# Batch 0's attention ahead of the first gate, value means on TensorE, weight subtraction on VectorE, and due times set from behind, in an attention and gated-expert kernel on one core

## The chip, the core and the metric

The kernel runs on one core of a Trainium2 chip. A core has five engines, each with its own queue of instructions that it runs in order: TensorE (PE, matmuls, with its weight loads shown as PEld), VectorE (DVE), ScalarE (ACT), GpSimd (POOL) and SyncE (SP, which here issues all DMAs). They share the on-chip memory SBUF; matmul results land in PSUM. Engines wait for each other by semaphores. The metric is the device time of one execution in microseconds; the number before is the median of three runs.

## The reference

Four batches of 768 tokens, 8 heads of 64. Each query attends to the keys within 16 positions of it and to 24 block summaries (maximum of 32 keys, mean of 32 values). The attention output, 512 features a token, then goes through a token mix, a squared-ReLU expert and a sigmoid gate.

```python
k_sum = k.reshape(B, H, nb, block, D).max(axis=3)
v_sum = v.reshape(B, H, nb, block, D).mean(axis=3)
mask_l = np.abs(pos[:, None] - pos[None, :]) < window
scores_s = scale * np.einsum('bhsd,bhnd->bhsn', q, k_sum) + np.log(block)
scores_all = np.concatenate([np.where(mask_l, scale * q @ kT, -1e9), scores_s], axis=-1)
a = softmax(scores_all)
x = a @ np.concatenate([v, v_sum], axis=2)
...
xk = mu_k * x + (1.0 - mu_k) * x_prev
xr = mu_r * x + (1.0 - mu_r) * x_prev
k = np.maximum(xk @ w_k, 0.0)
v = k * k @ w_v
r = 1.0 / (1.0 + np.exp(-(xr @ w_r)))
return r * v
```

## The kernel before

Work is cut into half batches of 384 tokens, written (b, hf), and four pairs of heads, p.

**Attention.** `load_set` issues the loads of a pair: keys `kt`, queries `qt`, value windows `vw`, and values with features on partitions, `vt`. `summaries` makes the block maxima of the keys on DVE (`kg`, `ks`, copied into `kt`), and the value means: a sum over `vt` on DVE (L327), a transpose on PE (L330), a scaled copy on ACT (`vm`, L332), and a DMA that spreads `vm` over the windows (L339). For batch 0 the loads and copies are made for each half separately, for the other batches once for both. `unit` is one pair and one half: 24 small score matmuls (L361), six times mask with row minimum on DVE (L372) and exponential with row sum on ACT (L376), the reciprocal of the sums on DVE (L382, L383), six scalings on POOL (L388), two groups of three transposes on PE (L395), each copied by ACT into `pts` (L399), 24 small value matmuls (L408), and a copy into `xt` on DVE (L419). There are 32 units, eight a batch.

**Weights.** They arrive as 64-bit words. For each of 20 blocks (4 of `w_r`, 8 each of `w_k` and `w_v`), `weight` loads `st` (L235), scales one word on ACT or POOL (L243, L246), takes bits from the other in two steps on DVE (L252, L255), joins them on DVE into `wc` (L260), casts that on ACT to the high part (L272), and subtracts on POOL to get the low part (L274). Products of a high and low operand are three matmuls: high-high, high-low, low-high.

**Tokens.** For each half, `mixes` makes high and low parts `xs` for the gate and then for the expert, four pairs each: ACT multiplies (L431), DVE adds (L434), ACT casts (L437), DVE subtracts (L439). `gate` is three tiles of 12 matmuls (L452 to L454) with a sigmoid on ACT each (L459). `experts` does eight steps j: `first` (`e1`, 12 matmuls at L472, which need weight block `wk` j; ReLU, square and a cast, then `kl` by subtraction on DVE, L487) and `second` (`e2`, 9 matmuls at L498, which need `wv` j, `kh` and `kl`). The last `e2` is followed by the product with the gate (L520) and the stores (L524).

**What sets the order.** Everything is first noted as an operation with an engine, a length from the table `LENGTH`, a due time and the buffers that it uses. `Plan.schedule` then plays the program forward: on each engine it takes, of the operations that can start, the one with the earliest due time, and so fixes the order of every engine's queue and which buffer of a pool each one gets. Nothing is reordered on the chip. Due times are written at each operation as offsets from the times of the half: the first gate is due at `T0`, each half `PERIOD` later, `e1` steps `STEP` apart. The four units of half (0,0) are due before the first gate, those of half (0,1) after it, and the eight units of the next batch during the two halves of this one.

```python
    for hf in range(2):
        for p in range(NPAIR):
            due = (16000 + 6000 * p) if hf == 0 else T0 + 4000 + 6000 * p
            e = load_set(0, p, hf * HW, HW, due)
            summaries(0, p, e, due)
            unit(0, p, hf, e, due)
```

## Time and profile before

| | |
|---|---|
| median of three runs | 493.21 us (491.12 to 852.7) |
| the profiled execution | 493.59 us, span 491.8 us |
| PE busy | 444.9 us, 90% of the span, 3376 matmuls |
| DVE busy | 295.0 us, 60% |
| ACT busy | 293.6 us, 60% |
| POOL busy | 119.8 us, 24% |
| chain that ended last | PE 70%, POOL 8%, ACT 7%, DVE 6%, DMA 5%, issue 3% |
| DMA | 42.82 MB read, 6.29 MB written, mean 106 GB/s |

The span is the time between the first and the last instruction in the trace. Busy times are averages over stages that have different limits, so the stages are read apart. The page cuts the span into 40 slices of 12.3 us; the digits are tenths of busy time. The lines for PE, DVE and POOL are these:

```profile
PE   1476988669889999999999999999999999999996
...
DVE  3879789999847676424677565526764654323223
...
POOL 0655346684512410001324120002343100000000
```

PE has its low slices at the left; DVE is at its fullest there, from the sixth slice to the tenth, and POOL too.

### The profile page before, as it was taken

How to read it: one execution, taken by the hardware profiler on the slowest of the kernel's cores; microseconds unless marked ns; L12 is line 12 of the kernel's file. 1: busy time of each engine (PE TensorE's matmuls, PEld its weight loads, DVE VectorE, ACT ScalarE, POOL GpSimd, SP SyncE). 2: the span in 40 equal slices, each digit the busy share in tenths (PEclk: the TensorE clock that was granted, in tenths of full speed). 3: DMA queues.
4: the chain of work that ended last, by engine and by line, in shares of the span. 5: the costliest groups of instructions: out<-in, count | busy, mean ns of one | idle time of the engine just before them, and what ended most of it. 6: DMA issues, size and time to landing. Idle time of an engine off the chain costs nothing.

```text
span 491.8 us, 9346 instructions
## 1 busy us (share of the span) xinstructions
PE 444.9 (90%) x3376; PEld 372.1 (76%) x3376; DVE 295.0 (60%) x914; ACT 293.6 (60%) x804; POOL 119.8 (24%) x228
## 2 busy tenths in 40 slices
PE   1476988669889999999999999999999999999996
...
DVE  3879789999847676424677565526764654323223
...
POOL 0655346684512410001324120002343100000000
...
GB/s 248 343 237 201 189 192 221 200 260 2 135 100 113 129 134 73 40 0 24 165 171 171 171 50 65 1 0 149 116 63 64 11 0 65 0 2 64 1 0 64
DMA packets 25501, 52.06 MB, mean 106 GB/s; under 512 B 2672, under 2 KB 12656, under 8 KB 25456
## 3 DMA queue, kind: packets, MB, share of 16 engines
...
HBM read 42.82 MB, written 6.29 MB: 100 GB/s over the span
## 4 chain that ended last, share of the span: by engine, by line
PE 70%; POOL 8%; ACT 7%; DVE 6%; DMA 5%; issue 3%; SPq 1%; DVEq 0%; POOLq 0%; ACTq 0%
PE mm L498 24%; PE mm L472 22%; POOL y L388 4%; PE mm L452 4%; PE mm L454 4%; PE mm L453 4%; PE av L408 4%; PE sc L361 4%; PE pt L395 4%; DMA kt<-in_k 3%; ACT y L376 2%; DVE we L255 1%; DMA vw<-vm 1%; POOL wv_l L274 1%; ACT L376 1%
## 5 line engine op out<-in xcount | busy, mean ns | idle before, releaser
L388 POOL TENSOR_SCALAR y<-y,rc 128x120 f32<-128x120 f32 x192 | 82.6, 449 | 249.0 <-DVE rc L383 197.1
L472 PE MATMUL mm<-xs,wk_h 128*128 128x384 f32 x512 | 102.3, 342 | 5.6 <-ACT r L478 4.3
L472 PEld LDWEIGHTS mm<-xs,wk_h 128*128 128x128 f32 x512 | 90.3, 189 | 10.7 <-ACT r L478 5.0
L376 ACT ACTIVATE y<-y,mn 128x120 f32<-128x120 f32 x192 | 73.8, 386 | 22.9 <-DVE mn L372 22.7
L478 ACT ACTIVATE r<-mm 128x384 f32<-128x384 f32 x64 | 31.3, 489 | 88.0 <-PE mm L472 87.6
L498 PE MATMUL mm<-wv_l,kh 128*128 128x512 f32 x192 | 76.9, 401 | 4.1 <-POOL wv_l L274 4.1
L498 PE MATMUL mm<-wv_h,kh 128*128 128x512 f32 x192 | 79.3, 413 | 0.0
L485 DVE CAST kh<-r 128x384 fp32r<-128x384 f32 x56 | 20.9, 374 | 88.7 <-ACT r L480 88.1
L498 PE MATMUL mm<-wv_h,kl 128*128 128x512 f32 x192 | 61.0, 413 | 0.3 <-DVE kl L487 0.3
L472 PE MATMUL mm<-xs,wk_l 128*128 128x384 f32 x256 | 55.3, 338 | 0.0
L439 DVE TENSOR_TENSOR xs<-xa,xs 128x384 fp32r<-128x384 f32 x64 | 36.2, 587 | 27.3 <-ACT xs L437 27.2
L372 DVE CUSTOM_DVE_ANT_0 y<-sc,mask_sb 128x120 f32<-128x120 f32 x192 | 44.1, 275 | 12.5 <-PE sc L361 11.9
L361 PE MATMUL sc<-kt,qt 64*64 64x120 f32 x768 | 33.1, 307 | 17.6 <-DVE kt L336 15.2
L472 PEld LDWEIGHTS mm<-xs,wk_l 128*128 128x128 f32 x256 | 45.5, 188 | 0.2
L395 PE MATMUL pt<-ident_sb,y 128*120 128x128 f32 x192 | 38.2, 308 | 8.0 <-POOL y L388 2.9
L498 PEld LDWEIGHTS mm<-wv_l,kh 128*128 128x128 f32 x192 | 36.6, 191 | 11.0 <-POOL wv_l L274 5.1
L361 PEld LDWEIGHTS sc<-kt,qt 64*64 64x64 f32 x768 | 24.1, 154 | 26.4 <-DVE kt L336 16.7
L498 PEld LDWEIGHTS mm<-wv_h,kh 128*128 128x128 f32 x192 | 36.8, 192 | 7.0 <-issue 0.6
L498 PEld LDWEIGHTS mm<-wv_h,kl 128*128 128x128 f32 x192 | 34.9, 192 | 8.6 <-DVE kl L487 0.8
L431 ACT ACTIVATE xa<-xt,om_sb 128x384 f32<-128x384 f32 x64 | 36.7, 608 | 7.6 <-DVE xt L419 6.6
L487 DVE TENSOR_TENSOR kl<-r,kh 128x384 fp32r<-128x384 f32 x64 | 37.1, 579 | 5.5 <-ACT kh L483 1.9
L434 DVE SCALAR_TENSOR_TENSOR xa<-xt,mu_sb,xa 128x384 f32<-128x384 f32 x64 | 38.1, 622 | 3.3 <-ACT xa L431 3.3
...
## 6 DMA issues: line engine op xcount, KB each, us to landing
...
```

The lines of the kernel that those rows point to most:

```text
L361: nc.tensor.matmul(sc[h].t[cs, i, 0:NK], qt.t[hs, w * QW:(w + 1) * QW], kt.t[hs, w * KB:w * KB + NK], start=True, stop=True,)
L372: op("DVE", "mask", due - 9000 + 300 * (NSL * h + i), lambda h=h, i=i, var=var: nc.vector.tensor_tensor_reduce(out=y[h].t[:, i, :], in0=sc ...
L376: op("ACT", "exp", due - 8500 + 300 * (NSL * h + i), lambda h=h, i=i: nc.scalar.activation(y[h].t[:, i, :], y[h].t[:, i, :], AF.Exp, bias= ...
L388: op("POOL", "norm", due - 5500 + 300 * (NSL * h + i), lambda h=h, i=i: nc.gpsimd.tensor_scalar(out=y[h].t[:, i, :], in0=y[h].t[:, i, :], ...
L395: nc.tensor.transpose(out=pt[h].t[0:NK, i * P:(i + 1) * P], in_=y[h].t[:, i, :], identity=ident_sb)
L431: op("ACT", "mixa", t - 4000, lambda xt=xt, xa=xa, p=p: nc.scalar.activation(xa.t, xt.t[:, lo:lo + HT], AF.Copy, scale=om_sb[:, which, p:p ...
L434: op("DVE", "mixd", t - 3300, lambda xt=xt, xa=xa, p=p: nc.vector.scalar_tensor_tensor(out=xa.t, in0=xt.t[:, 1 + lo:1 + lo + HT], scalar=m ...
L439: op("DVE", "sub", t - 1800, lambda xa=xa, xh=xh, xl=xl: nc.vector.tensor_tensor(out=xl.t, in0=xa.t, in1=xh.t.bitcast(F32), op=ALU.subtrac ...
L472: nc.tensor.matmul(ps.t[:, 0:HT], w[:, j, p, :], x[p][s].t, start=(n == 0), stop=(n == 11))
L478: op("ACT", "relu", due + 2200, lambda: nc.scalar.activation(r.t, ps.t[:, 0:HT], AF.Relu), reads=[(ps, 0)], writes=[(r, 0)])
L487: op("DVE", "sub", due + 3700, lambda: nc.vector.tensor_tensor(out=kl.t, in0=r.t, in1=kh.t.bitcast(F32), op=ALU.subtract), reads=[(r, 0), ...
L498: nc.tensor.matmul(acc[t].t, a.t[:, t * P:(t + 1) * P], w[:, j, :], start=start, stop=stop)
```

## The change

It has six parts.

1. **Batch 0 as a whole ahead of the first gate.** Each pair of batch 0 is loaded once for both halves, as in the other batches, and all eight units are due before the first gate (`GATES[0] - 2000`, 4000 ns apart). Queries come in a DMA of their own for each unit. In SP's list value windows go ahead of the mask.
2. **Value means of batch 0 by PE.** Twelve matmuls with a small constant matrix `pool_sb` (one more load) accumulate the 24 block means straight from the value windows, into a `mm` buffer. POOL first fills the rows of the windows that hold the means with zeros, since the matmuls read them. The load `vt`, the sum on DVE and the transpose are gone for batch 0; in the other batches they stay, with a `st` buffer for `vt`.
3. **The low part of a weight on DVE** in place of POOL, 20 subtractions of 128x512.
4. **Either of two engines.** An operation may name a second engine; the planner gives it to the one that ends it first. So the first step of a mix may go to POOL, the copy of the block maxima to POOL, the copy out of `av` to ACT, the cast of `kh` to ACT, the scaling of a weight to ACT or POOL.
5. **The gate of half (0,1) between steps of half (0,0).** Its `xs` are made early, and its three tiles stand in the program ahead of `e1` steps 1, 2 and 3.
6. **Dues from behind, and new numbers.** Only the operations of PE, the copies out of `av`, the last products and the stores keep a due time of their own; every other takes the earliest due time of what needs it, less its length and a slack. Loads aren't issued earlier than 15000 ns ahead of their due. The table of lengths is new, and the pools are cut differently (three `kt` in place of two, four `y` in place of six, three `pts` in place of four; windows and `xt` share twelve `vx`).

PE's matmuls are otherwise the same ones, in another order, and the number of activation table loads on ACT is the same, 24.

```diff
-LATENCY = dict(PE=260, DVE=130, ACT=150, POOL=150, SP=0)
-DMA_NS_PER_BYTE = 1 / 300.0
+TAIL = dict(PE=0, DVE=85, ACT=95, POOL=0, SP=0)
+LATENCY = dict(PE=260, DVE=110, ACT=110, POOL=150, SP=0)
+DMA_NS_PER_BYTE = 1 / 290.0
 DMA_FIXED = 2000
-T0 = 40000
+GATES = (36000, 46000)
 PERIOD = 52000
 STEP = 4800
+SLACK = 300
+EARLY = 15000
+FIRST = 4000
+UNITS = 6000
+BETWEEN = 1, 2, 3
...
+        ways = {eng: (LENGTH.get(cost, 0), emit)}
+        if other:
+            ways[other[0]] = (LENGTH[other[1]], other[2])
+        o = Op(len(self.ops), ways, due, bufs, size)
...
+        for o in reversed(self.ops):
+            own = 1.0e9 if o.due is None else o.due
+            wait = DMA_FIXED + o.size * DMA_NS_PER_BYTE if "SP" in o.ways else min(c for c, _ in o.ways.values()) + SLACK
+            o.due = min([own] + [s.due - wait for s in o.succ])
...
-                    start, need, ok = max(at, now), {}, True
+                    start, need, ok = max(at, now, o.due - EARLY if e == "SP" else 0), {}, True
...
+                    if any(max(start, engines[f]) + c < start + o.ways[e][0] for f, (c, _) in o.ways.items() if f != e):
+                        continue
...
-        kt=tiles("kt", 2, [P, KL]), qt=tiles("qt", 2, [P, S]), vw=tiles("vw", 2, [NK, NW, P]),
-        vt=tiles("vt", 1, [P, S]), kg=tiles("kg", 2, [P, 49]), ks=tiles("ks", NPAIR + 1, [P, NS]),
-        vs=tiles("vs", 2, [P, NS]), vm=tiles("vm", NPAIR + 1, [NS, P]),
-        y=tiles("y", 6, [P, NSL, NK]), mn=tiles("mn", 6, [P, NSL]), sm=tiles("sm", 4, [P, 2 * NSL]),
-        rc=tiles("rc", 4, [P, 2 * NSL]), pts=tiles("pts", 4, [NK, NSL, P]),
-        xt=tiles("xt", 7, [P, S + 1]), z=tiles("z", 2, [P, NTT, DM]),
-        xs=tiles("xs", 16, [P, HT], F32R), xa=tiles("xa", 4, [P, HT]),
-        r=tiles("r", 2, [P, HT]), kh=tiles("kh", 2, [P, HT], F32R), kl=tiles("kl", 2, [P, HT], F32R),
-        st=tiles("st", 3, [P, 1024], U32), wc=tiles("wc", 2, [P, 512], U32), we=tiles("we", 1, [P, 512], U32),
+        kt=tiles("kt", 3, [P, KL]), qt=tiles("qt", 4, [P, HT]), vx=tiles("vx", 12, [P, S + 1]),
+        kg=tiles("kg", 2, [P, 49]), ks=tiles("ks", 2, [P, NS]),
+        vs=tiles("vs", 1, [P, NS]), vm=tiles("vm", 4, [NS, P]),
+        y=tiles("y", 4, [P, NSL, NK]), mn=tiles("mn", 4, [P, NSL]), sm=tiles("sm", 3, [P, 2 * NSL]),
+        rc=tiles("rc", 3, [P, 2 * NSL]), pts=tiles("pts", 3, [NK, NSL, P]),
+        z=tiles("z", 6, [P, DM]), xa=tiles("xa", 4, [P, HT]),
+        xs=tiles("xs", 16, [P, HT], F32R), r=tiles("r", 2, [P, HT]),
+        kh=tiles("kh", 2, [P, HT], F32R), kl=tiles("kl", 2, [P, HT], F32R),
+        st=tiles("st", 3, [P, 1024], U32), we=tiles("we", 1, [P, 512], U32), wc=tiles("wc", 2, [P, 512], U32),
...
+        op("ACT", "wscale", None, scale_act, reads=[(st, 0)], writes=whole, other=("POOL", "wscale_p", scale_pool))
...
-        op("POOL", "sub_p", due - 1500, lambda: nc.gpsimd.tensor_tensor(
...
+        op("DVE", "wsub", None, lambda: nc.vector.tensor_tensor(
             out=dst_l, in0=wc.t.bitcast(F32), in1=dst_h.bitcast(F32), op=ALU.subtract),
-           reads=[(wc, 0), ((name, i), "h")], writes=[((name, i), "l")])
-
-
-    xts, key_sums, value_sums = {}, {}, {}
-
-    def load_set(b, p, w0, nw, due):
-
-        half = 1 if w0 else 0
-        e = dict(kt=buf("kt"), qt=buf("qt"), vw=buf("vw"), vt=None if half else buf("vt"), w0=w0, nw=nw)
-        first = w0 * KB
-        end = KL if half or nw == NW or b == 0 else first + nw * KB + 2 * WINDOW
-        kt, qt, vw = e["kt"], e["qt"], e["vw"]
-        cuts = [first, HW * KB, KL] if (b, p, w0) == (0, 0, 0) else [first, end]
+           reads=[*whole, ((name, i), "h")], writes=[((name, i), "l")])
...
+        op("DVE", "kcopy", None, copies(nc.vector), reads=[(ks, 0)], writes=[(kt, "s")],
+           other=("POOL", "kcopy_p", copies(nc.gpsimd)))
+        if b == 0:
+            tp = buf("mm")
+
+            for x in vw:
+                op("POOL", "fill", None, lambda x=x: nc.gpsimd.memset(x.t[QW:KB, 0:S], 0.0), writes=[(x, "b")])
+
+            def means():
+                for w in range(NW):
+                    nc.tensor.matmul(
+                        tp.t[0:NS, 0:P], pool_sb[:, NS - 2 - 2 * w:2 * NS - 2 - 2 * w], windows(vw[w // HW])[:, w % HW, :],
+                        start=(w == 0), stop=(w == NW - 1))
+
+            op("PE", "vpool", None, means, reads=[(x, y) for x in vw for y in "abc"] + [*POOLM], writes=[(tp, 0)])
...
+        for x in vw:
+            op("SP", "load", None, lambda x=x: nc.sync.dma_start(
+                out=windows(x)[QW:KB], in_=vm.t.unsqueeze(1).broadcast_to([NS, HW, P])),
+               reads=[(vm, 0)], writes=[(x, "b")], size=NS * HW * 512)
...
+        op("SP", "load", None, lambda: nc.sync.dma_start(out=qt.t, in_=q[b, p, :, hf * HT:(hf + 1) * HT]),
+           writes=[(qt, 0)], size=P * HT * 4)
...
+            op("POOL", "tiny", None, lambda: nc.gpsimd.memset(xt.t[:, 0:1], 0.0), writes=[(xt, "z")])
...
+           other=("ACT", "evac_a", lambda: nc.scalar.copy(out=xt.t[:, 1 + hf * HT:1 + (hf + 1) * HT], in_=av.t)))
...
+               other=("POOL", "mixa_p", lambda xt=xt, xa=xa, p=p: nc.gpsimd.tensor_scalar(
+                   out=xa.t, in0=xt.t[:, lo:lo + HT], scalar1=om_sb[:, which, p:p + 1], scalar2=1.0,
+                   op0=ALU.mult, op1=ALU.mult)))
...
+    def gate_tile(b, hf, x, z, t):
+        ps = buf("mm")
+        ts = slice(t * P, (t + 1) * P)
+
+        def products():
+            for p, (xh, xl) in enumerate(x):
+                nc.tensor.matmul(ps.t, xh.t[:, ts], wr_h[:, p, :], start=(p == 0), stop=False)
+                nc.tensor.matmul(ps.t, xh.t[:, ts], wr_l[:, p, :], start=False, stop=False)
+                nc.tensor.matmul(ps.t, xl.t[:, ts], wr_h[:, p, :], start=False, stop=(p == NPAIR - 1))
+
+        op("PE", "gate", gate_due(b, hf) + 2800 * t, products, reads=[(a, 0) for pair in x for a in pair]
+           + [(("wr", i), s) for i in range(NCK) for s in "hl"], writes=[(ps, 0)])
+        op("ACT", "sigmoid", None, lambda: nc.scalar.activation(z[t].t, ps.t, AF.Sigmoid),
+           reads=[(ps, 0)], writes=[(z[t], 0)])
...
-            if b == 0 and hf == 0:
-                op("ACT", "cast", due + 3200, lambda: nc.scalar.copy(out=kh.t, in_=r.t), reads=[(r, 0)], writes=[(kh, 0)])
-            else:
-                op("DVE", "khv", due + 3200, lambda: nc.vector.tensor_copy(out=kh.t, in_=r.t),
-                   reads=[(r, 0)], writes=[(kh, 0)])
-            op("DVE", "sub", due + 3700, lambda: nc.vector.tensor_tensor(
+            op("DVE", "khv", None, lambda: nc.vector.tensor_copy(out=kh.t, in_=r.t),
+               reads=[(r, 0)], writes=[(kh, 0)], other=("ACT", "cast", lambda: nc.scalar.copy(out=kh.t, in_=r.t)))
...
+            for work in between.get(j, ()):
+                work()
...
-    for hf in range(2):
-        for p in range(NPAIR):
-            due = (16000 + 6000 * p) if hf == 0 else T0 + 4000 + 6000 * p
-            e = load_set(0, p, hf * HW, HW, due)
-            summaries(0, p, e, due)
-            unit(0, p, hf, e, due)
...
+    for p in range(NPAIR):
+        e = load_set(0, p)
+        for h in range(2):
+            unit(0, p, h, e, GATES[0] - 2000 - (7 - 2 * p - h) * FIRST)
+    tokens = {}
+    for n in range(2 * B):
+        b, hf = divmod(n, 2)
+        if n not in tokens:
+            tokens[n] = mixes(b, hf, 1), [buf("z") for _ in range(NTT)]
+            for t in range(NTT):
+                gate_tile(b, hf, *tokens[n], t)
+        between = {}
+        x = mixes(b, hf, 0)
+        if n == 0:
+
+            tokens[1] = mixes(0, 1, 1), [buf("z") for _ in range(NTT)]
+            between = {j: [lambda t=t: gate_tile(0, 1, *tokens[1], t)] for t, j in enumerate(BETWEEN)}
+        experts(b, hf, x, tokens[n][1], between)
...
+    means = np.zeros((NK, 2 * NS - 2), np.float32)
+    means[WINDOW:WINDOW + BLOCK, NS - 2] = 1.0 / BLOCK
+    means[WINDOW + BLOCK:QW, NS - 1] = 1.0 / BLOCK
+    means[KB:KB + WINDOW, NS - 1] = 1.0 / BLOCK
```

What this does to the order of the queues, at three places. First PE around the first gate (`sc` scores, `pts` and `av` values, `y` and `pt` transposes, `mm` with `wr` the gate, with `wk` the first `e1`). Before, where the last work ahead of the gate, the end of the gate and the first `e1` stand:

```order
L408 MATMUL av0_150<-pts0_102,vw0_65 64x64
...
L361 MATMUL sc1_148<-kt0_61,qt0_63 64x120 x2
L452 MATMUL mm0_151<-wr_h_163,xs0_115 128x512
L453 MATMUL mm0_151<-wr_l_164,xs0_115 128x512
...
L454 MATMUL mm2_153<-wr_h_163,xs7_122 128x512
L395 MATMUL pt0_149<-ident_sb_156,y4_86 120x128 x3
L472 MATMUL mm3_154<-xs8_123,wk_h_159 128x384
...
L395 MATMUL pt0_149<-ident_sb_156,y5_87 120x128 x3
```

and now, with the second gate's first tile that follows the first `e1`:

```order
L430 MATMUL pt0_146<-ident_sb_153,y2_91 120x128 x3
L430 MATMUL pt0_146<-ident_sb_153,y3_92 120x128 x3
...
L443 MATMUL av0_147<-pts0_103,vx10_78 64x64
L489 MATMUL mm0_148<-wr_h_160,xs0_116 128x512
L490 MATMUL mm0_148<-wr_l_161,xs0_116 128x512
...
L510 MATMUL mm3_151<-xs14_130,wk_l_157 128x384
L396 MATMUL sc0_144<-kt1_62,qt0_64 64x120 x2
...
L489 MATMUL mm0_148<-wr_h_160,xs0_116 128x512
...
L510 MATMUL mm1_149<-xs8_124,wk_h_156 128x384
```

Ahead of the gate stood seven scores, ten groups of transposes and five values; now eight scores, sixteen groups, eight values and the four mean products stand there, and the transposes of batch 0 that stood among the first `e1` are gone from there.

Second DVE in the middle of the weights (`we` and `wc` the steps of a block, `y` a mask). Before:

```order
L252 TENSOR_SCALAR we_146<-st_141 128x512
L255 SCALAR_TENSOR_TENSOR we_146<-st_141,we_146 128x512
L260 SCALAR_TENSOR_TENSOR wc_145<-wc_145,we_146 128x512
L372 ISA y_87,mn_93<-sc_148,mask_sb 128x120
...
L252 TENSOR_SCALAR we_146<-st_142 128x512
L255 SCALAR_TENSOR_TENSOR we_146<-st_142,we_146 128x512
L487 TENSOR_TENSOR kl_140<-r_136,kh_138 128x384
```

and now:

```order
L275 TENSOR_SCALAR we_141<-st_139 128x512
L407 ISA y_90,mn_94<-sc_145,mask_sb 128x120
...
L278 SCALAR_TENSOR_TENSOR we_141<-st_139,we_141 128x512
L292 TENSOR_TENSOR wv_l<-wc_142,wv_h 128x512
L282 SCALAR_TENSOR_TENSOR wc_143<-wc_143,we_141 128x512
```

The three steps of a block stood one behind the other; now other work stands between them, the subtraction of the block before (L292) among it.

Third the head of SP's queue (`vx` value windows of pair 0). Before:

```order
L290 DMA kt_61<-in_k 128x528
L290 DMA kt_61<-in_k 128x560
L294 DMA qt_63<-in_q 128x384
L212 DMA mask_sb<-in_mask 128x360
L213 DMA mu_sb<-in_mu 128x8
```

and now:

```order
L308 DMA kt_61<-in_k 128x560
L308 DMA kt_61<-in_k 128x528
L379 DMA qt_64<-in_q 128x384
L312 DMA vx_68<-in_v 64x768
L312 DMA vx_69<-in_v 64x768
L315 DMA vx_68<-in_v 32x768
L315 DMA vx_69<-in_v 32x768
L236 DMA pool_sb<-in_pool 120x46
L234 DMA mask_sb<-in_mask 128x360
```

The mask moved from the fourth place to the ninth, behind the windows of the first pair; the load of `mu` moved from the fifth place to the thirty-seventh.

More of the change, by code (lines that the diff above doesn't have):

```diff
@@ new lines, in weight @@
+        op("SP", "load", None, load, writes=[(st, 0)], size=P * 4096)
+        op("ACT", "wscale", None, scale_act, reads=[(st, 0)], writes=whole, other=("POOL", "wscale_p", scale_pool))
+        op("DVE", "wbits", None, low, reads=[(st, 0)], writes=[(we, 0)])
+        op("DVE", "wor", None, sign, reads=[(st, 0), (we, 0)], writes=[(we, 0)])
+        op("DVE", "wor", None, join, reads=[(we, 0), *whole], writes=whole)
+        op("ACT", "wcast", None, lambda: nc.scalar.copy(out=dst_h, in_=wc.t.bitcast(F32)),
+           reads=whole, writes=[((name, i), "h")])
```

285 lines of the change are left out of this document (130 added, 155 removed).

## The prediction

> **What bounds the kernel now.** I read the table of busy time by stage first, then PE's timeline, then VectorE's (DVE) and GpSimd's (POOL) timelines where PE waits, then the grouped lines for prices. In the table a row is a stretch, its length, the busy time of PE, its weight loads, DVE, ACT and POOL with instruction counts, the granted clock, the DMA share and GB/s. The cuts are the first gate (53.66), the first `e1` (63.70), the end of half (0,0) (129.30) and the first gates of batches 1, 2 and 3.
>
> ```profile
> 0.00:53.66 53.66, 28.56 (x322) 20.38 (x322) 39.47 (x145) 28.06 (x102) 21.95 (x44) 1.00 0.82 254
> ...
> 63.70:129.30 65.60, 51.28 (x392) 40.48 (x389) 58.24 (x131) 45.82 (x122) 40.09 (x45) 0.95 0.52 166
> 129.30:190.63 61.33, 58.35 (x523) 48.67 (x523) 39.20 (x140) 46.27 (x128) 15.20 (x36) 0.97 0.44 128
> 190.63:296.20 105.57, 105.25 (x846) 89.42 (x845) 61.89 (x215) 68.36 (x193) 20.27 (x48) 1.00 0.32 95
> 296.20:401.81 105.61, 105.28 (x845) 89.50 (x844) 57.23 (x202) 68.25 (x193) 17.81 (x48) 1.00 0.18 55
> 401.81:491.80 89.99, 86.12 (x418) 75.60 (x416) 31.12 (x62) 29.42 (x58) 0.00 (x0) 0.99 0.07 27
> ```
>
> From 190.63 on PE works without a hole (105.25 of 105.57, 105.28 of 105.61), and the change leaves its products there as they are; so the last 491.8 - 190.6 = 301.2 us stay. The room lies ahead: PE is idle 25.1 us before the first gate, 14.3 in half (0,0), 3.0 in half (0,1).
>
> PE's rows give start, length, line, tiles, count, and in brackets the idle time before and its releaser.
>
> ```profile
> 5.90 1.48 PE L361 MATMUL sc<-kt,qt 64*64 64x120 f32 x24 [5.90 <-DVE kt L336]
> ...
> 24.24 1.55 PE L408 MATMUL av<-pts,vw 120*64 120x64 f32 x24
> ...
> 28.08 0.87 PE L395 MATMUL pt<-ident_sb,y 128*120 128x128 f32 x3 [0.66 <-ACT pts L399]
> 28.88 1.48 PE L361 MATMUL sc<-kt,qt 64*64 64x120 f32 x24
> ...
> 46.20 1.55 PE L408 MATMUL av<-pts,vw 120*64 120x64 f32 x24
> 47.68 0.90 PE L395 MATMUL pt<-ident_sb,y 128*120 128x128 f32 x3
> 49.29 0.86 PE L395 MATMUL pt<-ident_sb,y 128*120 128x128 f32 x3 [0.71 <-POOL wc L246]
> ...
> 50.78 1.54 PE L408 MATMUL av<-pts,vw 120*64 120x64 f32 x22 [0.22 <-ACT pts L399]
> 52.25 1.48 PE L361 MATMUL sc<-kt,qt 64*64 64x120 f32 x24
> 53.66 0.79 PE L452 MATMUL mm<-wr_h,xs 128*128 128x512 f32 x1
> ...
> 110.54 0.50 PE L498 MATMUL mm<-wv_l,kh 128*128 128x512 f32 x1 [2.62 <-POOL wv_l L274]
> ...
> 116.59 0.85 PE L361 MATMUL sc<-kt,qt 64*64 64x120 f32 x24
> 117.36 0.92 PE L408 MATMUL av<-pts,vw 120*64 120x64 f32 x24
> 118.21 1.68 PE L472 MATMUL mm<-xs,wk_h 128*128 128x384 f32 x8
> ```
>
> Two things are seen. Before the first gate the small matmuls take nearly twice their later time, although the granted clock reads 1.00: scores 1.41 us to the next start (52.25 to 53.66) against 0.77 (116.59 to 117.36), values 1.48 (46.20 to 47.68) against 0.85. Three transposes take 0.80 (28.08 to 28.88). And in half (0,0) PE waits for weights (the 2.62 at 110.54). Why those are late is in the rows of DVE and POOL:
>
> ```profile
> 51.54 0.56 DVE L439 TENSOR_TENSOR xs<-xa,xs 128x384 fp32r<-128x384 f32 x1 [0.24 <-ACT xs L437]
> ...
> 59.08 0.56 DVE L439 TENSOR_TENSOR xs<-xa,xs 128x384 fp32r<-128x384 f32 x1 [1.98 <-ACT xs L437]
> ...
> 70.70 0.80 DVE L487 TENSOR_TENSOR kl<-r,kh 128x384 fp32r<-128x384 f32 x1 [1.48 <-ACT kh L483]
> ...
> 91.00 0.55 DVE L487 TENSOR_TENSOR kl<-r,kh 128x384 fp32r<-128x384 f32 x1
> 91.47 0.68 DVE L260 SCALAR_TENSOR_TENSOR wc<-wc,we 128x512 uint32<-128x512 uint32 x1
> 92.07 0.27 DVE L372 CUSTOM_DVE_ANT_0 y<-sc,mask_sb 128x120 f32<-128x120 f32 x1
> ...
> 92.27 0.42 DVE L252 TENSOR_SCALAR we<-st 128x512 uint32<-128x512 uint32 x1
> 92.73 0.69 DVE L255 SCALAR_TENSOR_TENSOR we<-st,we 128x512 uint32<-128x512 uint32 x1
> 93.52 1.57 DVE L260 SCALAR_TENSOR_TENSOR wc<-wc,we 128x512 uint32<-128x512 uint32 x1
> ...
> 95.21 0.68 DVE L252 TENSOR_SCALAR we<-st 128x512 uint32<-128x512 uint32 x1
> ...
> 123.90 0.60 DVE L487 TENSOR_TENSOR kl<-r,kh 128x384 fp32r<-128x384 f32 x1 [0.42 <-ACT kh L483]
> ```
> ```profile
> 92.89 1.65 POOL L274 TENSOR_TENSOR wv_l<-wc,wv_h 128x512 fp32r<-128x512 f32 x1 [1.90 <-DMA st<-in_w_v]
> 94.63 0.98 POOL L246 TENSOR_SCALAR wc<-st 128x512 f32<-128x512 f32 x1
> ```
> ```profile
> L255 DVE SCALAR_TENSOR_TENSOR we<-st,we 128x512 uint32<-128x512 uint32 x20 | 19.0, 948 | 0.6
> L260 DVE SCALAR_TENSOR_TENSOR wc<-wc,we 128x512 uint32<-128x512 uint32 x20 | 18.6, 930 | 2.3 <-POOL wc L246 0.9 <-ACT wc L243 0.6
> L520 DVE TENSOR_TENSOR z<-mm,z 128x512 f32<-128x512 f32 x24 | 16.6, 691 | 5.8 <-PE mm L498 5.5
> L252 DVE TENSOR_SCALAR we<-st 128x512 uint32<-128x512 uint32 x20 | 11.6, 580 | 0.0
> ```
>
> The join that starts at 93.52, inside POOL's subtraction (92.89 to 94.54), lasts 1.57 against 0.68 at 91.47. The means carry it: 948, 930 and 580 ns against 0.69, 0.68 and 0.42 undisturbed, together 0.67 us for each of 20 weight blocks. So half (0,0) is bound by DVE, and POOL's subtractions make DVE slower.
>
> **The start, up to the first gate.** Moved ahead of the gate are three scores, three values and six transpose groups of batch 0; new are four mean products of 12 matmuls each; gone are four sums `vs` on DVE. PE's list before the gate, at the rates above: 8 scores x 1.41 = 11.3, 8 values x 1.48 = 11.8, 16 transpose groups x 0.80 = 12.8. A mean product has no row. One matmul streams 128 columns; three transposes of 128 columns give 0.27 each as the nearest row, the warm rate of the scores (0.77 / 6 groups of four tiles, 0.13) the lower end, and if the four tiles of a score don't overlap fully, twice 0.25 the upper. I take 0.25, so 12 x 0.25 = 3.0 us each, 12 for four (6 to 24). Sum 47.9. Between 46.20 and 53.66 PE stood still for 0.71 and 0.22, so it was 87.5% filled; with that and the first score at 5.9 the gate starts at 5.9 + 47.9 / 0.875 = 60.6 (54 to 72, rivals A and C). This is 7 later than now, for three units more. DVE is not what ends last there: it is busy 39.47 of 53.66, and the list gains 12 masks, two weight blocks and five subtractions and loses four `vs`, about +5 us. The loads are covered: up to the last broadcast of the means SP's list holds some 9.6 MB, at the row's 254 GB/s 38 us. The mask, now ninth on the queue behind 1.4 MB, lands after some 8 us; the first masks wait for it about 1 us, while PE does the first mean product.
>
> **Half (0,0), now with the gate of (0,1) in it.** From the end of the fourth `xs` (51.54 + 0.56) to the eighth `kl` (123.90 + 0.60) are 72.4 us. DVE's list between the same two points changes by: 15 subtractions, priced by the 128x512 product at L520 less its overlap, 0.65 each (0.61 to 0.69): +9.8; two weight trios fewer (0.46 + 0.79 + 0.60): -3.7; seven `xs` at 0.47 and two mixes at 0.53 for the early gate: +4.4; 17 masks fewer at 0.20: -3.4; the small rest about -1. Net +6. POOL's 16 subtractions go: 16 x 0.67 = -10.7. With other work between the steps of a trio the second takes 0.60 in place of 0.79, the first 0.40: 13 x 0.27 = -3.5. POOL gets some eight other instructions there (mixes, copies, scalings); beside the scaling at 94.63 a 0.42 step took 0.68, so 8 x 0.26 = +2.1. Of DVE's 6.5 us of waits (1.98 and 1.48 in the rows) I let half go, since the new lengths are near the rows: -3. Sum 72.4 + 6 - 10.7 - 3.5 + 2.1 - 3 = 63.3 (56 to 69). PE's list there is the first gate, the gate of (0,1), eight `e1` and `e2`, three scores. The last two halves have nothing else on PE: 86.12 less two gates, halved, is 34.7 for a half's `e1` and `e2`, if a gate is 8.4 (rows below). So PE has 34.7 + 16.8 + 2.3 = 53.8 us to do in 63.3: DVE still ends last and the gate of (0,1) hides in PE's gaps; had DVE no load there, its 8.4 us would show.
>
> The Trainium skill, "SBUF — State Buffer", section "Who interferes with whom", says that a DVE instruction with two SBUF inputs and a GpSimd instruction that reads SBUF exclude each other for the whole instruction. The stretched join agrees (1.57). The rule speaks against the new mixes on POOL: by it eight such instructions could cost up to 8 x 0.65 = 5.2 in place of 2.1, and the sum would be 3 us more.
>
> **Half (0,1).** The gate is gone from here.
>
> ```profile
> 144.91 1.27 PE L408 MATMUL av<-pts,vw 120*64 120x64 f32 x22 [2.02 <-ACT pts L399]
> ...
> 401.85 0.40 PE L452 MATMUL mm<-wr_h,xs 128*128 128x512 f32 x1
> ...
> 404.65 0.40 PE L498 MATMUL mm<-wv_h,kh 128*128 128x512 f32 x1
> ```
>
> A gate tile is 2.80 (401.85 to 404.65), three are 8.4. From above: from the eighth `kl` (124.5) to 190.63 are 66.1 us; less the gate 8.4, less the first `e1` of (0,1), issued ahead of the eighth `e2` now, 2.2, less the 2.0 wait at 144.91, plus one score, one values and two transpose groups that come later than now, 2.1: 55.6. From below: PE's work after the eighth `kl` is 34.7 and five scores, eight values, fifteen transpose groups at the later rates, 3.9 + 6.8 + 15 x 0.25 = 14.4: 49.1, and the row's idle time of 3.0 makes 52.1. I take the middle, 54.
>
> **Sum.** 60.6 + 63.3 + 54.0 + 301.2 = 479.1 span; the profiled execution took 493.59 for its span of 491.8, so 480.9. The median is 493.21, 0.4 less; I leave that.
>
> **Rivals.** (A) PE runs the start at its full rate. Then its list halves and DVE's 39.5 + 5 = 44.5 ends last: 58.7 with all of the present 14.2 of gaps, 50 with only the wait for the first loads (about 5.5); the middle is 54: 474. Against: from 46.20 to 53.66 PE is nearly filled and its rows still are 1.55 and 1.48. The skill's "TensorE: Matmul & The Clock Gate", Part 1, has the full clock after some 3.4 us of sustained activity; that rule would give this case, and the rows there disagree. (B) DVE's waits vanish and PE bounds half (0,0): 56 in place of 63.3, 474; with (A) 467. (C) The change doesn't shorten: units keep their pace, first values at 24.24, fifth at 50.78, 6.6 us each, with two `y` pairs in flight in place of three; the eighth would end at 24.2 + 7 x 6.6 + 1.5 = 72, 492. Against: the last gap is 4.6 (46.20 to 50.78). (D) Slower: the three gate tiles between the `e1` steps hold the ACT queue. Their sigmoids stand ahead of weight casts, the tile waits in PE's order behind an `e1` that waits for a weight. At a step (6.5 us) each that is some 20 us: 501; from 4 us each nothing is won.
>
> **How the numbers follow.** My case 0.47, its own range 473 to 489; A 0.17, B 0.13, C 0.15, D 0.08. A measurement tells about 2% apart, the line is 483.3. My case lies below it with 0.26 of its 0.47; with A and B faster is 0.56; the rest of it and C give 0.36 for the same; D 0.08 for slower. The range 465 to 495 reaches from A with B to C.
>
> **What would show it.** The first gate near 60 with scores still at 1.4 before it (right), or near 54 with scores at 0.8 (A), or near 72 (C). The joins at 0.6 to 0.7 with none at 1.5; from first gate to eighth `kl` 63, DVE without long waits. The gate of batch 1 near 178 and 301 us behind it. I am wrong if PE waits before `e2` on casts of ACT (D), or if the last three batches change by more than 3 us.

## The result, and the profile after

The changed kernel took 479.89 us (median of four runs, 479.43 to 480.32) against 492.95 for the kernel before: a ratio of 0.9747, 95% interval 0.9718 to 0.9776. It is 2.5% faster, where 480.9 was forecast. The ratio leaves out one run of the kernel before, of 852.7 us; its other three lie between 491.12 and 493.21. The profiled execution has a span of 478.5.

The table of busy time by stage, of the changed kernel (length, busy time of PE, its weight loads, DVE, ACT and POOL, granted clock, DMA share, GB/s). The cuts are its first gate, the end of the eighth low part `kl`, and the first gates of batches 1, 2 and 3:

```profile
0.00:61.54 61.54, 44.93 (x528) 33.70 (x528) 42.47 (x169) 39.42 (x141) 36.25 (x71) 0.82 0.73 209
61.54:125.90 64.36, 57.62 (x316) 48.16 (x316) 55.95 (x127) 51.44 (x104) 15.69 (x23) 0.93 0.62 190
125.90:178.22 52.32, 52.32 (x531) 44.02 (x530) 32.72 (x128) 38.52 (x128) 17.38 (x40) 1.00 0.16 45
178.22:281.91 103.69, 103.27 (x836) 87.76 (x835) 55.98 (x197) 65.17 (x189) 26.79 (x61) 1.00 0.35 102
281.91:387.89 105.98, 105.56 (x846) 89.35 (x844) 57.91 (x201) 67.86 (x195) 26.14 (x60) 1.00 0.33 84
387.89:478.50 90.61, 86.53 (x418) 75.42 (x416) 30.33 (x59) 28.49 (x56) 3.16 (x3) 0.99 0.07 27
```

Set beside the forecast: start 61.5 (60.6), half (0,0) to the eighth `kl` 64.4 (63.3), half (0,1) 52.3 (54.0), the rest 478.50 - 178.22 = 300.3 (301.2). Before, the four were 53.7, 70.8 (53.66 to 124.50), 66.1 and 301.2. So the start gave back 7.9 us, the halves won 6.5 and 13.8, the rest 0.9. In the page's 40 slices (now of 12.0 us) PE reads 8 or more from the eighth on (84 us), where before it did so from the tenth (111 us), and it is full from the tenth where it was from the thirteenth (108 and 148 us):

```profile
PE   4878797889999999999999999999999999999996
...
DVE  2669997779955486527454566429355564222223
...
POOL 5527903205135402301433302202242302000000
PEclk9987589799999999999999999999999999999999
```

The last line is the granted clock in tenths: the two slices from 36 to 60 us read 7 and 5. In the old start it was 1.00 throughout.

PE's rows of the start (start, length, then idle time before with its releaser) show something else that is new:

```profile
5.60 1.48 PE L396 MATMUL sc<-kt,qt 64*64 64x120 f32 x24 [5.60 <-DVE kt L337]
8.05 4.94 PE L350 MATMUL mm<-vx,pool_sb 120*24 120x128 f32 x24 [0.98 <-DMA pool_sb<-in_pool]
12.92 0.85 PE L396 MATMUL sc<-kt,qt 64*64 64x120 f32 x24
...
18.23 2.80 PE L350 MATMUL mm<-vx,pool_sb 120*24 120x128 f32 x24 [1.06 <-DMA vx<-in_v]
...
46.93 1.48 PE L396 MATMUL sc<-kt,qt 64*64 64x120 f32 x24
```

The first mean product takes 4.94 us, the later ones 2.80 (3.0 was forecast), and the scores behind it run in 0.85, where the kernel before needed 1.48 for each of them. From 38 us on two of them are at 1.48 again, now where the granted clock is low.

The joins and their neighbours are no longer stretched, as the groups by line show (count, busy, mean ns, idle before). The first two are those of the whole program, the eight subtractions of the third lie in half (0,0):

```profile
L278 DVE SCALAR_TENSOR_TENSOR we<-st,we 128x512 uint32<-128x512 uint32 x20 | 14.5, 723 | 0.1
L282 DVE SCALAR_TENSOR_TENSOR wc<-wc,we 128x512 uint32<-128x512 uint32 x20 | 14.4, 718 | 0.2
L292 DVE TENSOR_TENSOR wv_l<-wc,wv_h 128x512 fp32r<-128x512 f32 x8 | 5.9, 735 | 6.3 <-ACT wv_h L290 6.3
```

The means fell from 948 and 930 ns to 723 and 718. But the third row has a wait that the forecast did not have: DVE stands 6.3 us before three of its new subtractions, for ACT's cast (and 1.5 us more before one of the `wk`). ACT's timeline at the longest of them, then the rows of DVE and PE that wait there:

```profile
78.28 1.28 ACT L411 ACT_TABLE_LOAD   x1
79.57 0.40 ACT L411 ACTIVATE y<-y,mn 128x120 f32<-128x120 f32 x1
79.88 0.19 ACT L411 ACTIVATION_READ_ACCUMULATOR y<-y,mn 128x1 f32 x1
80.08 1.28 ACT L495 ACT_TABLE_LOAD   x1
81.37 0.60 ACT L495 ACTIVATE z<-mm 128x512 f32<-128x512 f32 x1
81.99 1.28 ACT L411 ACT_TABLE_LOAD   x1
...
83.68 0.60 ACT L290 CAST wv_h<-wc 128x512 fp32r<-128x512 f32 x1
```
```profile
84.31 0.69 DVE L292 TENSOR_TENSOR wv_l<-wc,wv_h 128x512 fp32r<-128x512 f32 x1 [3.48 <-ACT wv_h L290]
85.47 0.79 PE L489 MATMUL mm<-wr_h,xs 128*128 128x512 f32 x1 [2.71 <-ACT r L515]
```

Exponential (L411) and sigmoid (L495) need different activation tables, and the sigmoids of the early gate now stand between exponentials. One sigmoid of 0.60 us brings two loads of 1.28, the cast of a weight stands behind them, and DVE waits 3.48 us. The whole program has 22 loads (24 before; the section on the change says 24 for both, which was too many for the new one), but half (0,0) has 8 of them where it had 4.

### The profile page after: what moved, and what is told of

The parts are those of the page before. It is cut to its first block, busy times and chain, and to the rows that moved or that the text cites. A ratio compares the mean times of both kernels' runs of the same rounds, so it can differ in the third digit from the quotient of the medians.

```text
span 478.5 us, 9637 instructions
## 1 busy us (share of the span) xinstructions
PE 450.2 (94%) x3468; PEld 378.4 (79%) x3468; DVE 275.4 (58%) x876; ACT 290.9 (61%) x810; POOL 125.4 (26%) x258
## 4 chain that ended last, share of the span: by engine, by line
PE 77%; ACT 6%; DVE 2%; issue 1%; POOL 1%; POOLq 0%; ACTq 0%
PE mm L531 27%; PE mm L510 26%; PE mm L489 4%; PE av L443 4%; PE mm L490 4%; PE mm L491 4%; PE pt L430 4%; PE sc L396 3%; ACT y L411 2%; ACT L411 1%; POOL y L423 1%; ACT L495 1%; ACT wc L268 1%; DVE wc L282 0%; ACT wv_h L290 0%
## 5 line engine op out<-in xcount | busy, mean ns | idle before, releaser
L423 POOL TENSOR_SCALAR y<-y,rc 128x120 f32<-128x120 f32 x192 | 87.2, 472 | 173.2 <-DVE rc L418 154.7
L510 PE MATMUL mm<-xs,wk_h 128*128 128x384 f32 x512 | 101.1, 339 | 2.0 <-ACT r L515 1.1
L411 ACT ACTIVATE y<-y,mn 128x120 f32<-128x120 f32 x192 | 73.7, 386 | 13.4 <-DVE mn L407 13.2
L531 PE MATMUL mm<-wv_l,kh 128*128 128x512 f32 x192 | 75.7, 394 | 0.0
L519 DVE CAST kh<-r 128x384 fp32r<-128x384 f32 x39 | 14.9, 382 | 73.6 <-ACT r L517 73.3
L477 DVE TENSOR_TENSOR xs<-xa,xs 128x384 fp32r<-128x384 f32 x64 | 34.8, 553 | 22.2 <-ACT xs L475 22.0
L489 PE MATMUL mm<-wr_h,xs 128*128 128x512 f32 x96 | 40.5, 422 | 2.7 <-ACT r L515 2.7
L472 DVE SCALAR_TENSOR_TENSOR xa<-vx,mu_sb,xa 128x384 f32<-128x384 f32 x64 | 40.4, 653 | 4.5 <-POOL xa L469 4.1
L430 PE MATMUL pt<-ident_sb,y 128*120 128x128 f32 x192 | 36.3, 298 | 7.0 <-ACT pts L434 5.8
L434 ACT COPY pts<-pt 120x384 f32<-120x384 f32 x64 | 30.2, 472 | 20.2 <-PE pt L430 20.2
L490 PE MATMUL mm<-wr_l,xs 128*128 128x512 f32 x96 | 39.2, 409 | 0.0
```

The costliest lines, as they stand in the source:

```text
L411: op("ACT", "exp", None, lambda h=h, i=i: nc.scalar.activation(y[h].t[:, i, :], y[h].t[:, i, :], AF.Exp, bias=mn[h].t[:, i:i + 1], scale=-1.0,
L423: op("POOL", "norm", None, lambda h=h, i=i: nc.gpsimd.tensor_scalar(out=y[h].t[:, i, :], in0=y[h].t[:, i, :], scalar1=rc.t[:, NSL * h + i: ...
L430: nc.tensor.transpose(out=pt[h].t[0:NK, i * P:(i + 1) * P], in_=y[h].t[:, i, :], identity=ident_sb)
L472: op("DVE", "mixd", None, lambda xt=xt, xa=xa, p=p: nc.vector.scalar_tensor_tensor(out=xa.t, in0=xt.t[:, 1 + lo:1 + lo + HT], scalar=mu_sb ...
L477: op("DVE", "sub", None, lambda xa=xa, xh=xh, xl=xl: nc.vector.tensor_tensor(out=xl.t, in0=xa.t, in1=xh.t.bitcast(F32), op=ALU.subtract), ...
L489: nc.tensor.matmul(ps.t, xh.t[:, ts], wr_h[:, p, :], start=(p == 0), stop=False)
```

## The experiments

Ratios are to the kernel before, measured beside each. Stages as above, in us, from one profiled execution each.

| run | ratio (95% interval) | start | half (0,0) | half (0,1) | rest |
|---|---|---|---|---|---|
| before | 1 | 53.7 | 70.8 | 66.1 | 301.2 |
| changed kernel | 0.9747 (0.9718 to 0.9776) | 61.5 | 64.4 | 52.3 | 300.3 |
| e1 subtraction on POOL again | 1.0039 (1.0008 to 1.0069) | 62.6 | 73.7 | 54.3 | 300.5 |
| e2 before, subtraction on DVE | 0.9900 (0.9863 to 0.9938) | 46.3 | 68.0 | 65.7 | 302.8 |
| e3 gate of (0,1) late | 0.9728 (0.9669 to 0.9786) | 60.8 | 51.3 | 59.7 | 302.7 |
| e4 tanh | 0.9616 (0.9555 to 0.9677) | 62.3 | 57.0 | 52.2 | 298.3 |
| e5 tanh, gate late | 0.9620 (0.9564 to 0.9676) | 61.7 | 50.3 | 59.3 | 300.5 |
| e6 units of (0,1) due later, gate late | 1.0116 (1.0067 to 1.0165) | 78.4 | 49.8 | 63.4 | 302.4 |
| e7 short mean products | one run | 59.9 | 64.1 | 52.3 | 300.3 |
| e8 narrow unpacking | one run | 60.5 | 64.5 | 52.3 | 300.4 |
| e9 narrow scalings | one run | 59.5 | 64.1 | 52.8 | 300.0 |
| e10 mixes and weight scalings off POOL | 0.9616 (0.9553 to 0.9679) | 56.7 | 64.2 | 52.8 | 299.8 |
| e11 tanh, scalings on POOL or ACT | 0.9611 (0.9551 to 0.9671) | 57.5 | 63.8 | 50.0 | 300.0 |
| e12 e4 and e10 together | 0.9564 (0.9494 to 0.9634) | 61.6 | 57.7 | 52.4 | 297.9 |

### The weight subtraction

Edit of e1, made in the changed kernel, with 1300 ns for it in the planner's table of lengths (e2 makes the opposite one in the kernel before):

```diff
-        op("DVE", "wsub", None, lambda: nc.vector.tensor_tensor(
+        op("POOL", "wsub_p", None, lambda: nc.gpsimd.tensor_tensor(
             out=dst_l, in0=wc.t.bitcast(F32), in1=dst_h.bitcast(F32), op=ALU.subtract),
```

> The changed kernel with the weight subtraction on POOL again, as before the change, all else kept. The prediction's terms price the move at +9.8 for the subtractions on DVE against -10.7 for the stretched steps, so about nothing: half (0,0) (first gate to end of the eighth low part kl) stays at 64.4 within 2 us, the time at 478 to 482, with joins of 1.5 us back on DVE. Rival: what counts is that POOL's subtraction takes 1.65 us in place of 0.69 in the line from cast to product, and holds the word buffer longer: 13 blocks in half (0,0) at 0.5 to 1 us each, 6 to 13 us, time 486 to 493.

> The kernel before with only the weight subtraction moved to DVE. By the prediction's terms DVE's list in half (0,0) changes by +9.8 - 10.7: the time stays within 1.5 us of the kernel before (492 to 494). Rival (latency of POOL's subtraction counts): half (0,0) gets 6 us or more shorter, 486 or less. Third case: DVE, which bounds this half, gets the work without the stretched steps going away fully, 496 or more.

With the subtraction back on POOL the whole gain is gone (1.0039), in half (0,0) for the most part. The stage's row of e1, the groups of the two joining steps of a weight, and those of two operations that are no part of a weight:

```profile
62.55:136.27 73.72, 60.22 (x307) 49.53 (x307) 63.18 (x120) 46.86 (x96) 42.52 (x42) 0.87 0.53 167
```
```profile
L278 DVE SCALAR_TENSOR_TENSOR we<-st,we 128x512 uint32<-128x512 uint32 x12 | 13.3, 1110 | 0.0
L477 DVE TENSOR_TENSOR xs<-xa,xs 128x384 fp32r<-128x384 f32 x13 | 12.4, 957 | 0.0
L282 DVE SCALAR_TENSOR_TENSOR wc<-wc,we 128x512 uint32<-128x512 uint32 x13 | 11.1, 852 | 0.3 <-POOL wc L271 0.3
L472 DVE SCALAR_TENSOR_TENSOR xa<-vx,mu_sb,xa 128x384 f32<-128x384 f32 x12 | 8.9, 761 | 0.0
```

The same groups of the changed kernel in its half (0,0):

```profile
L278 DVE SCALAR_TENSOR_TENSOR we<-st,we 128x512 uint32<-128x512 uint32 x13 | 9.2, 708 | 0.0
L282 DVE SCALAR_TENSOR_TENSOR wc<-wc,we 128x512 uint32<-128x512 uint32 x13 | 9.2, 707 | 0.0
L472 DVE SCALAR_TENSOR_TENSOR xa<-vx,mu_sb,xa 128x384 f32<-128x384 f32 x10 | 6.7, 687 | 0.4 <-ACT xa L466 0.4
L477 DVE TENSOR_TENSOR xs<-xa,xs 128x384 fp32r<-128x384 f32 x12 | 6.3, 550 | 0.0
```

DVE is busy 63.2 us in e1 and 55.95 in the changed kernel, though the latter has 15 subtractions more on it (5.9 + 4.8 us). POOL's subtractions stretch not the weight steps alone: the `xs` take 957 ns in place of 550. By the means the four groups cost some 13 us more in e1 (4.8 and 1.9 for the weight steps, 5.3 for the `xs`, 0.9 for the mixes), against 10.7 that leave DVE; and the half holds two mixes, three copies and other steps of DVE more, some 3 us.

In the kernel before, where half (0,0) held 6 `xs` in place of 12, the same move leaves DVE's busy time in this half where it was, as the forecast's +9.8 and -10.7 say (62.80 before, 63.00 in e2), and the time falls by 1.0%: the first gate comes 7.3 us earlier, with less of PE's work ahead of it (245 matmuls in place of 322), and the half is 2.9 shorter. So the move is worth 1.0% by itself and 0.9747 against 1.0039, 2.9%, within the rest of the change.

For e2 the measured 1.0% (488 on the scale of 493) lies between the cases that were set out, for e1 the rival's 486 to 493 came out by the number (492.7 as measured; on the scale of 493 it is 494.9). Its mechanism, the latency, was not tested by itself, but the trace of e1 speaks for the stretch and these steps: of the 9.3 us that half (0,0) is longer, 7.2 are busy time of DVE, and neither DVE nor PE has a wait there for a low part from POOL. ACT waits 2.4 us for POOL to let go of the word buffer, and 1.9 for DVE in the changed kernel.

### The early gate and the activation tables

Edit of e3: the list of steps is empty, the due time of that gate is the usual one, and its `xs` are no longer made early. Edit of e4:

```diff
-        op("ACT", "sigmoid", None, lambda: nc.scalar.activation(z[t].t, ps.t, AF.Sigmoid),
+        op("ACT", "sigmoid", None, lambda: nc.scalar.activation(z[t].t, ps.t, AF.Tanh, scale=0.5),
...
-            op("ACT", "square", None, lambda: nc.scalar.activation(r.t, r.t, AF.Square),
+            op("ACT", "square", None, lambda: nc.scalar.activation(r.t, r.t, AF.Square, scale=0.5**0.5),
...
-                op("DVE", "result", due + 4000 + 700 * t, lambda t=t: nc.vector.tensor_tensor(
-                    out=z[t].t, in0=acc[t].t, in1=z[t].t, op=ALU.mult),
+                op("DVE", "result", due + 4000 + 700 * t, lambda t=t: nc.vector.scalar_tensor_tensor(
+                    out=z[t].t, in0=z[t].t, scalar=1.0, in1=acc[t].t, op0=ALU.add, op1=ALU.mult),
```

> The changed kernel with the gate of half (0,1) in its old place, behind half (0,0). Prediction: the gate hides in PE's gaps, so taking it out leaves half (0,0) at 64 and adds 8.4 behind it: 488. Rival (activation tables): its three sigmoids stand between exponentials and cost three pairs of table loads of 1.28 us, which the chain of waits of half (0,0) shows five times; without them the half is 5 to 8 us shorter, and the time 480 to 483.

> The changed kernel with the sigmoid written as half of one plus the hyperbolic tangent of half the argument: the factor of one half goes into the square, the one into the last product. The order of all queues is the same; the table loads fall from 24 to 1. If table loads lie on the line that sets the end of half (0,0) (five of 1.28 us in its chain of waits): half (0,0) 58, time 472 to 475. If DVE's list bounds the half, as predicted, the loads are hidden: half (0,0) 62 to 64, time 478 to 480.

> The changed kernel with the gate of half (0,1) behind half (0,0) again and the hyperbolic tangent in place of the sigmoid. With the tanh alone half (0,0) took 57.0 us with DVE busy in 56.0 of them, with the late gate alone 51.3 with 49.8. If DVE's list alone bounds both, the tables left in the late version are hidden: half (0,0) 49 to 51, and the gate's 8.4 us on PE comes back behind it, so that this is level with the tanh alone within 1% (ratio to the kernel before 0.953 to 0.971). Rival: once the tables are gone, the gate between the steps is worth the 8.4 us of PE that it was meant to hide: this is 5 to 8 us slower than the tanh alone (ratio 0.972 to 0.978).

The rows of half (0,0) in e4, e3 and e5, in this order:

```profile
62.31:119.27 56.96, 55.83 (x317) 47.07 (x317) 55.98 (x127) 41.22 (x96) 18.38 (x23) 0.97 0.68 209
```
```profile
60.79:112.08 51.29, 46.17 (x278) 38.85 (x278) 49.84 (x117) 39.74 (x89) 17.71 (x23) 0.98 0.76 226
```
```profile
61.66:111.93 50.27, 45.73 (x277) 38.44 (x277) 49.66 (x117) 37.28 (x87) 18.00 (x23) 0.98 0.76 229
```

With the tanh one table load is left in the program, ACT has 10.2 us less to do in the half (51.44 to 41.22), and the half is 7.4 us shorter. The order of the queues is the same. DVE has the same 55.98 us, now 98% of the stage, and PE's 55.83 fill it as far; with the gate late DVE fills 97 and 99% of it, PE 90 and 91. So both readings hold, one behind the other: DVE's list is a bound, which PE's reaches too when the gate is early, and of the 8.4 us of waiting on top (64.36 - 55.95) the table loads make 7.4. In the order of e10 the same edit takes 6.4 us from this half (64.2 to 57.7, e12). The Trainium skill, "ScalarE: Activation LUTs", section "Table sets: the hidden batching unit", has exponential and tanh in one set, so that going from one to the other needs no load; the trace of e4 agrees, with one load in all.

On the scale of 493 e3 took 479.6, just below both of its cases, e4 474, the case of the table loads; e5 came out level with e4, as when DVE's list bounds both. The early gate gains nothing: with the sigmoid 0.9747 early and 0.9728 late, with the tanh 0.9616 and 0.9620. Early it takes 7.1 us from half (0,1) (59.3 to 52.2), and late it takes 6.7 from half (0,0) (57.0 to 50.3), since DVE's part of it, 56.0 - 49.7 = 6.3 us, moves along. And in e5 PE has gaps of 50.27 - 45.73 = 4.5 us in this half, for 10.1 us of work that the early gate adds (45.7 to 55.8). A product that was to hide in PE's gaps was not free: the gaps were too short for it, and what prepares it runs on the engine that makes them.

### What ends the start

Four experiments shorten one engine's list at a time. e7 has `for w in range(0, NW, 4)` in the mean products; e8 the columns `0:64` of 512 in the three steps of the gate's weight; e9 the columns `0:24` of 120 in the scalings; e10 leaves out the second engine of the mixes' first step and of the weight scalings.

> The changed kernel with 3 of the 12 matmuls in each of the four mean products of batch 0, so that the block means lack nine windows of twelve; all queues else as in the changed kernel. PE's list before the gate gets shorter by 0.75 of 4.94 + 3 x 2.80, 10 us. If PE's list ends the start, as predicted, the first gate comes at 50 to 53. If DVE does (busy in 25.2 of the last 26.5 us before the gate), it stays within 1.5 us of 61.5.

> The changed kernel with the three DVE steps that unpack a block of the gate's weight done on 64 of 512 columns, so that the other columns of these four blocks keep a wrong value; all queues else as in the changed kernel. DVE's list before the gate gets shorter by 4 x (0.35 + 0.60 + 0.60), 6 us, all of it in the last 30 us. If DVE ends the start, the first gate comes at 55 to 57. If PE's list does, as predicted, it stays within 1.5 us of 61.5.

> The changed kernel with each scaling by the reciprocal sums on POOL done on 24 of 120 columns, so that the other columns stay unscaled; all queues else as in the changed kernel. Shortening PE's list by 10 us and DVE's by 6 moved the first gate by only 1.6 and 1.0 us. Theory: POOL sets the pace of the start; from 40.5 to 59.8 us its rows leave 0.5 us idle and its scalings take up to 0.76 us each beside DVE. Then the first gate comes 5 us or more earlier, at 56 or before. Rival: no one engine sets it, but the loads up to 35 us and the latency of one unit with two in flight: less than 2.5 us, 59 or later.

> The changed kernel without two of its choices of engine: the first step of a mix and the scaling of a weight go to ACT always, as nothing but the scalings of a unit and the copies is then left to POOL before the first gate. If POOL sets the pace of the start, the first gate comes 2 to 4 us earlier (its three mixes and four weight scalings there take 7 us), and in half (0,0), where ACT waits on table loads, ACT's 6 us more make it 0 to 4 us longer: ratio to the kernel before 0.965 to 0.978. If POOL does not set it: first gate at 61 or later, ratio 0.976 to 0.99.

e7: PE's list got shorter by less than planned, since with mean products of 1.45 us the scores stayed slow up to 27 us. Its rows:

```profile
8.46 1.45 PE L350 MATMUL mm<-vx,pool_sb 120*24 120x128 f32 x6 [0.43 <-DMA pool_sb<-in_pool]
...
14.76 1.48 PE L396 MATMUL sc<-kt,qt 64*64 64x120 f32 x24
...
19.68 1.48 PE L396 MATMUL sc<-kt,qt 64*64 64x120 f32 x24
```

PE's busy time up to the gate is 40.7 in place of 44.9, and the gate came 1.6 us earlier. It is a test of less than it was meant to be; but it shows what the long mean products do besides: the scores behind them run in 0.85, behind the short ones in 1.48, at a granted clock of 1.00 in both (0 to 20 us). The Trainium skill's "TensorE: Matmul & The Clock Gate", Part 1, has the full clock after some 3.4 us of sustained activity. The mean product of 4.94 us agrees; but small matmuls without a gap, 5.9 us of them from 17.45 in e7 and 4.7 from 31.15 in the kernel before, stayed slow, while in e7 the rows turned fast between 27.1 and 28.0, 3 to 4 us after a gap that ended at 24.2. So the length of a stretch without gaps alone doesn't decide it. What else counts, no run here shows.

e8 moved the gate by 1.0 us, e9 by 2.0, the case of its rival (59 or later). Up to the gate the changed kernel, e3, e4 and e5 have the same queues, and their gates lie between 60.8 and 62.3; e8 is 0.3 us below this range, e7 0.9, e9 1.3, with one run each. In e9 POOL's scalings did not get short with their width: the last four groups of six took 2.11, 2.83, 2.39 and 4.51 us with 24 columns, 3.05, 3.68, 3.90 and 4.54 with 120. So its list fell by 4.7 us only from 35 us on, and the theory's 5 us were not to be had from it.

e10, which takes seven instructions from POOL, moved the gate by 4.8, more than the 2 to 4 expected. Its half (0,0) has four table loads in place of eight and more steps on ACT, and stays at 64.2; DVE still waits there, 5.1 us of it for ACT's casts. The stretch from 35 us to the gate in the changed kernel, in e10, and in e12, whose queues up to the gate are the same as those of e10 (the rest of it is told below):

```profile
35.00:61.54 26.54, 21.39 (x246) 15.48 (x246) 25.24 (x87) 22.22 (x77) 21.50 (x31) 0.63 0.55 166
```
```profile
35.00:56.70 21.70, 15.01 (x247) 10.87 (x244) 18.39 (x71) 21.06 (x74) 12.61 (x24) 0.97 0.36 118
```
```profile
35.00:61.62 26.62, 23.00 (x235) 16.94 (x231) 18.44 (x68) 21.65 (x71) 12.14 (x24) 0.50 0.30 93
```

The second and third have the same work on DVE (18.4), ACT (21 to 22) and POOL (12 to 13); PE needs 15.0 us for it at a granted clock of 0.97 and 23.0 at 0.50, and the gate is at 56.7 and 61.6. In e10 ACT is 97% filled. In e12 PE is the fullest with 86% (ACT has 81%), so PE's list is the likeliest to end the start there. In the changed kernel DVE is filled to 95%, with POOL and PE at 81% each, and in e3, at a clock of 0.84 there, the gate is at 60.8, only 0.7 earlier; in e8, with DVE filled to 82%, it is at 60.5. So no one list alone ends its start, and in e7 to e9 shortening one alone wins 2 us at most; which chain ends it was not found. What sets the granted clock was not tried, and e10 and e12 ran on different chips; with one profile of each kernel e10's earlier gate may be owed to it in part.

e6, made with the late gate of e3, was to put only the units of half (0,0) ahead of the gate. The line that does it:

```diff
-            unit(0, p, h, e, GATES[0] - 2000 - (7 - 2 * p - h) * FIRST)
+            unit(0, p, h, e, GATES[0] - 2000 - (6 - 2 * p) * FIRST if h == 0 else GATES[0] + 8000 + p * UNITS)
```

> The changed kernel with the late gate (as in the run with the late gate) and with only the four units of half (0,0) due before the first gate, those of half (0,1) behind it, as before the change. If moving the units only shifts time from one stage to another: first gate at 44 to 50 in place of 60.8, half (0,0) and half (0,1) longer by 10 to 14 together, time within 1% of the late-gate run (ratio to the kernel before 0.963 to 0.983). If moving the units is what the change lives from: ratio 0.99 or more. Third: the early units cost more than they give, ratio 0.955 or less.

Its 1.0116 lies in the range of the second case, but it doesn't tell this: all eight units still stand ahead of the gate, in a worse order, and the gate comes at 78.4. The buffers of a pool are given out in the order in which the program is written, pair by pair, so that a unit of the second half holds the turn of the next pair's first. What the move of the units is worth by itself stays open, and so does the share of the mean products on PE, of the second engines and of the due times.

### Two versions that go further

> The changed kernel with the hyperbolic tangent in place of the sigmoid, and with ACT as second engine for the scalings of a unit that POOL does (with 600 in place of 455 in the table of lengths, so that about a third of them go to ACT). If POOL sets the pace of the start: first gate at 54 to 58 in place of 62.3, and the time 4 to 8 us below that of the tanh alone (ratio to the kernel before 0.945 to 0.953). If it does not, level with the tanh alone (0.955 to 0.968).

> The changed kernel with the hyperbolic tangent in place of the sigmoid and with the mixes' first step and the weight scalings on ACT always. The run without these two choices brought the first gate to 56.7 and left half (0,0) at 64.2; the tanh alone left the gate at 62.3 and brought half (0,0) to 57.0. If the two lie in different stages and add up: gate at 56 to 58, half (0,0) at 56 to 59, ratio to the kernel before 0.942 to 0.953. Rival: with ACT taking 13 scalings and ten mixes, ACT's list becomes the bound of half (0,0) and gives back what the tables gave: half (0,0) 61 or more, ratio 0.957 or more.

e11 brought the gate to 57.5, but half (0,0) back to 63.8: DVE is busy 60.6 there and waits again, so the tanh's gain was lost, by which of the moved instructions was not tried; the ratio, 0.9611, lies in the range of the second case. e12 kept half (0,0) at 57.7 with DVE busy in 57.54, and took 470.04 us against 491.92, a ratio of 0.9564: the fastest of these, but its interval overlaps with those of e4 and e10, and the expected sum (0.942 to 0.953) was missed, its profiled execution having the start at 61.6 and the low clock. Its four runs took 468.5 and 468.6 us at a mean granted clock of 0.98, 471.5 and 473.3 at 0.96 to 0.97.

## Why the prediction was right

**The start, 60.6 forecast, 61.5 measured.** The list of PE was sized well, for partly wrong reasons. PE's groups up to the gate:

```profile
L350 PE MATMUL mm<-vx,pool_sb 120*24 120x128 f32 x96 | 13.3, 305 | 2.0 <-DMA vx<-in_v 1.1 <-DMA pool_sb<-in_pool 1.0
L443 PE MATMUL av<-pts,vx 120*64 120x64 f32 x192 | 12.4, 274 | 2.3 <-ACT pts L434 1.8 <-DMA vx<-vm 0.5
L430 PE MATMUL pt<-ident_sb,y 128*120 128x128 f32 x48 | 12.0, 359 | 6.1 <-ACT pts L434 5.8 <-POOL y L423 0.3
L396 PE MATMUL sc<-kt,qt 64*64 64x120 f32 x192 | 9.1, 325 | 6.2 <-DVE kt L337 5.6 <-DVE mn L407 0.6
```

Mean products, values, transposes and scores sum to 46.8, against 47.9. The scores were costed at the slow rate throughout; four of the eight ran at 0.85 or 0.84, and the mean products cost 1.3 more. That PE's list is what ends the start may hold at the low clock of e12 alone; in the changed kernel DVE, which "is not what ends last there", is 95% filled at the end of it. Rival A was half there: PE ran most of its work from 13 to 35 us at full rate, and the gate still did not come at 54.

**Half (0,0), 63.3 forecast, 64.4 measured.** DVE ends last, as forecast, but two terms were off against each other. The sum had 3.5 of DVE's 6.5 us of waits left, so about 60 us of work; measured were 56.0 of work and 8.4 of waits. Some of the work was never there: in the 72.4 us that the sum starts from DVE was busy for 64.1 and stood for 8.3, of which the sum counts 6.5 as waits. And freeing DVE from POOL also shortened the `xs`, from 692 to 550 ns each, which the term "POOL's 16 subtractions go: 16 x 0.67" does not hold; the mixes got no shorter (638 and 687). The rest of the difference was not taken apart. The waits are more because of the table loads around the early sigmoids: 7.8 of the 8.4 us are for ACT's casts of weights. This is rival D in kind, sigmoids that hold the ACT queue; it was priced at a step (6.5 us) for each of three, and cost 7.4 us in all. The forecast's sign of it, PE waiting before `e2` on casts, did not show: PE's one long wait there, 2.0 us, was for a sigmoid, and it was DVE that waited for the casts. The subtraction, worth -0.9 net in the forecast's sum, weighs more: without it the rest of the change gains nothing, with it 2.9% (e1).

**Half (0,1), 54.0 forecast, 52.3 measured.** It lies at the bound from below (52.1): PE works without a gap (52.32 of 52.32). The 8.4 us of the gate did leave it, but e3 and e5 show that half (0,0) paid for them.

**The last part, 301.2 forecast, 300.3 measured.** Unchanged, as forecast.

The four parts are off by +0.9, +1.1, -1.7 and -0.9 us and the sum by -0.6. That it is so close is in part luck: the range of the forecast was wide, the stages were sized by terms that erred both ways, and the drop of the clock in the start was not in it.
